# Seven stretches of TensorE's order with leads of their own, in an attention and gated-MLP kernel with packed results and three blocks of maxima on ScalarE and GpSimd

## The chip, the core and the metric

The kernel runs on one core of one Trainium2 chip. A core has TensorE (PE in the profile; PEld is its loading of weights), VectorE (DVE), ScalarE (ACT), GpSimd (POOL) and SyncE (SP), which here issues every DMA. The engines work beside each other and wait for one another through semaphores. Each runs its own instructions in the order in which they were written. The metric is the device time of one execution in microseconds, given as the median of several runs.

## What is computed

A sequence of 2048 tokens of 512 features is normalised, and the result goes both into attention with 32 heads of 16 features and into a gated MLP of width 1792. Both results and the input are added.

```python
def _A_ref(x, wqkv, wo):
    B, S, D = x.shape
    H = 32
    Dh = D // H
    qkv = (lambda x, *d: x.transpose(*d))((x @ wqkv).reshape(B, S, 3, H, Dh), 2, 0, 3, 1, 4)
    q, k, v = qkv[0], qkv[1], qkv[2]
    scores = jnp.einsum("bhqd,bhkd->bhqk", q, k) * (Dh ** -0.5)
    p = _softmax(scores, axis=-1)
    o = jnp.einsum("bhqk,bhkd->bhqd", p, v)
    return (lambda x, *d: x.transpose(*d))(o, 0, 2, 1, 3).reshape(B, S, D) @ wo

def _B_ref(x, w1, w3, w2):
    gate = jnp.einsum("bsd,df->bsf", x, w1)
    up = jnp.einsum("bsd,df->bsf", x, w3)
    h = _silu(gate) * up
    out = jnp.einsum("bsf,fd->bsd", h, w2)
    return out

x = A_x
xn = _layernorm(x, axis=-1)
return x + _A_ref(xn, A_wqkv, A_wo) + _B_ref(xn, B_w1, B_w3, B_w2)
```

## The kernel before

**Tiling.** The 32 heads form 8 groups of four, and the 2048 queries four chunks of 512. A *unit* is one chunk, one group and 256 queries of it, or 128 at the very start and in the last four groups. There are 73 units, 0 to 72, and they are worked in order. A head has 16 features, and each head of a group stands in 32 partitions of its own, so that TensorE works on the four heads in four row groups.

**The two passes over the scores.** The softmax subtracts each row's exact maximum, so the scores are computed twice.

- In the first pass, `p1_cand` (L1052), TensorE computes a *block*: 128 queries against 512 keys for two heads, into two PSUM banks. VectorE reduces the block to two columns of maxima (`part`, L1101). There are 1024 blocks, 16 for a unit of 256 queries. Banks 0 to 3 hold two blocks in turn.
- When a unit's blocks are done, `final_max` makes the row maxima. GpSimd does it in six small operations (L1209 to L1216), or VectorE in one reduction for the first three and the last eight units (L1239). GpSimd then writes the negated maxima into `Z` (L1186, L1188). For most units a transposing DMA makes `Zs` of them, and four small DMAs put the rows beside the queries in `QZ` (L1228). The queries themselves come into `QZ` by four more DMAs (L1061), issued when the units that used the place are through. For the first three and some of the last units TensorE and ScalarE do it instead (tile AQ, L803).
- In the second pass, `p2_cand` (L1344), TensorE computes the scores again, this time with the maximum subtracted by two further rows of the product. ScalarE takes the exponential of a bank of 512 columns into a slot of `PT` (L1360), or of two banks in one instruction (`exp_pair`, L1390). A unit of 256 queries has 32 such tiles, one of 128 has 16.

**Results.** `tile_PV` (L574) multiplies the exponentials with the values. Each head's 16 result rows are followed by a row of sums of the exponentials, and the rest of its 32 partitions is unused. ScalarE copies this to `U` (L1455). A chain normalises it, one unit at a time: a DMA takes the sums out (Lc), GpSimd raises them to the power of -1 (L1480), two DMAs spread the reciprocals over the partitions through DRAM (rd, R), and GpSimd multiplies (L1500) into `onorm`. For the last three units (`FAST_PV`) TensorE also multiplies with ones, and VectorE does a reciprocal and a product (L1445, L1447) instead.

**Output.** `tile_OUT` adds, in one PSUM bank for 128 tokens, the input, 14 products of the MLP and one product for each of the 8 groups with `wo`, whose rows are spread in the same way with zeros between. ScalarE copies the bank out (L912). The last four tiles are split: OUTA holds all but the groups' products, and OUTB those (L588); VectorE adds the two (L957). The MLP's tiles G and U are followed by three ScalarE instructions (L844 to L850) and three of GpSimd (L828 to L833).

**The order.** `_build` simulates the engines with its own costs and writes all instructions in the order it finds. In each step each engine offers its best candidate, and the earliest one is emitted. For TensorE, `pick_pe` weighs a block of the first pass (a), a tile of the second (b) and a matmul of a column tile (c: results, projections, MLP, output). A block is due `A_LEAD` before VectorE will have finished its work, and a score tile `ROW_LEAD` before ScalarE's queue is empty. What isn't due gives way to column work. `COUPLE` lets two of them go together, `RELAX` delays tiles of the second pass, `PAIR_WAIT` is how long ScalarE may wait for a pair, and `PV_LEFT` is how many exponentials of a unit may be open when its results begin. When there is no column work and TensorE's recent load is low, a filler is put in: a product of the identity and `xnT` into a free bank. Work may also be forced ahead when the recent load is too low for the clock. `K.at(LEADS.get(...))` sets these leads anew every 32 blocks (`STRETCH`). `LEADS` is empty, so they are the same throughout. VectorE takes its queue `redq` in order; the last units' reciprocals and OUTB's additions go into the same queue.

## Time and profile before

| | |
|---|---|
| median of 3 runs | 1202.11 us (1200.79 to 1204.87) |
| span of the profiled execution | 1199.6 us |
| VectorE busy, share of the span | 1181.7 us, 99% |
| ScalarE | 1168.2 us, 97% |
| TensorE | 1118.9 us, 93% |
| GpSimd | 442.0 us, 37% |
| granted TensorE clock, mean | 0.998 |

The span is the time from the first to the last instruction on the core; the runs' times lie a little above it. A row of the timeline or the chain begins with the start and the length in us; the number in brackets is the idle time of the engine just before, and what ended it. In the windows view a row is the stretch, its length, the engines' busy time, the granted clock, the DMA share and GB/s. A group row has the busy time and the mean length in ns, then the idle time before. The length of a VectorE or ScalarE instruction overlaps the next one's start, so what counts for a full engine is the pitch, from start to start.

### The profile page before, as it was taken

To read this page: it belongs to the slowest core of one execution; us is meant where nothing else is said; L and a number is where in the kernel's file an instruction comes from. 1 tells how busy PE (TensorE), PEld (TensorE's weight loads), DVE (VectorE), ACT (ScalarE), POOL (GpSimd) and SP (SyncE) were. 2 spreads that over 40 slices of the span, in tenths; PEclk is the share of its full clock that TensorE was granted. 3 is DMA by queue.
4 is the path that set the end of the run, shared out by engine and by line. 5 is a ranking of instruction groups with operands and counts; after the bars stand their busy time and mean duration, and the time that the engine had idled before them with its cause. 6 is when DMAs were issued, how large, how long until landed. Compare 5 with 4: busy or idle time off the path is not lost.

```text
span 1199.6 us, 32809 instructions
## 1 busy us (share of the span) xinstructions
PE 1118.9 (93%) x13295; PEld 489.5 (41%) x13451; DVE 1181.7 (99%) x1087; ACT 1168.2 (97%) x2249; POOL 442.0 (37%) x855
## 2 busy tenths in 40 slices
PE   8999999999899999999999999999999999898997
PEld 3433334334334433333434433433333444345554
DVE  9999999999999999999999999999999999999995
ACT  7879999999999999999999999999999999999997
POOL 3254645532222156542222154356532222233220
PEclk9999999999999999999999999999999999999999
DMA  6523223211011122210001121022110200000000
GB/s 185 120 59 83 70 53 91 58 49 30 20 26 31 42 56 48 55 42 23 24 21 30 33 64 44 24 49 61 39 27 20 59 24 24 20 19 14 13 11 23
DMA packets 136756, 53.54 MB, mean 45 GB/s; under 512 B 102189, under 2 KB 136605, under 8 KB 136605
## 3 DMA queue, kind: packets, MB, share of 16 engines
q1 hardware_dynamic: 136604, 51.44, 17.2%
q8 instruction: 106, 1.74, 0.6%
q14 instruction: 46, 0.37, 0.1%
HBM read 38.86 MB, written 6.74 MB: 38 GB/s over the span
## 4 chain that ended last, share of the span: by engine, by line
ACT 47%; PE 27%; DVE 22%; issue 2%; POOL 1%; DMA 1%; another core or an unknown queue 0%
ACT PT L1360 35%; DVE part L1101 21%; PE ps L588 9%; PE ps L1344 8%; ACT PT L1390 6%; PE ps L574 6%; PE ps L1052 4%; ACT th L844 1%; ACT U L1455 1%; ACT zg L846 1%; ACT ub L850 1%; ACT kq L750 1%; DVE t L615 1%; DVE hT L648 0%; DMA R<-rd 0%
## 5 line engine op out<-in xcount | busy, mean ns | idle before, releaser
L1101 DVE TENSOR_REDUCE part<-ps 128x2 f32<-128x1024 f32 x1024 | 1160.1, 1212 | 1.4 <-PE ps L1344 1.0
L1360 ACT ACTIVATE PT<-ps 128x512 bf16<-128x512 f32 x1714 | 908.8, 651 | 6.4 <-PE ps L1344 2.9
L1344 PE MATMUL ps<-QZ,KT 32*128 32x256 bf16 (+1 forms) x3456 | 526.2, 273 | 15.4 <-ACT PT L1390 5.1
L1052 PE MATMUL ps<-KT,QT 32*128 32x512 bf16 x2048 | 402.2, 385 | 8.4 <-DVE part L1101 4.2
L1344 PEld LDWEIGHTS ps<-QZ,KT 32*128 32x128 bf16 (+1 forms) x3456 | 200.7, 93 | 191.2 <-ACT PT L1360 71.3
L1480 POOL TENSOR_TENSOR Rc<-Lc,mone 128x8 f32<-128x8 f32 (+1 forms) x70 | 105.9, 1513 | 239.9 <-DMA Lc<-U 239.8
L574 PE MATMUL ps<-PT,Vaug 128*17 128x256 bf16 (+1 forms) x4672 | 176.5, 261 | 4.9 <-ACT PT L1390 1.1
L1390 ACT ACTIVATE PT<-ps 128x1024 bf16<-128x1024 f32 x167 | 174.5, 1092 | 1.4 <-PE ps L1344 1.1
L588 PE MATMUL ps<-xnT,w 128*128 128x512 bf16 (+1 forms) x528 | 144.3, 339 | 14.0 <-ACT zg L846 4.8
L1052 PEld LDWEIGHTS ps<-KT,QT 32*128 32x128 bf16 x2048 | 98.5, 91 | 138.7 <-DVE part L1101 80.2
L588 PE MATMUL ps<-xnT,ident 128*128 128x256 bf16 (+1 forms) x400 | 129.4, 345 | 17.6 <-ACT PT L1390 6.9
L574 PEld LDWEIGHTS ps<-PT,Vaug 128*17 128x17 bf16 x4672 | 85.8, 89 | 80.0 <-issue 56.3
L831 POOL TENSOR_TENSOR a<-zg,ub 128x512 f32<-128x512 bf16 x56 | 64.6, 1154 | 72.5 <-ACT ub L850 72.5
L588 PEld LDWEIGHTS ps<-xnT,ident 128*128 128x128 bf16 x484 | 42.3, 96 | 103.5 <-ACT PT L1360 53.8
L1344 PE MATMUL ps<-QT,KT 32*128 32x128 bf16 (+1 forms) x1216 | 80.8, 220 | 3.1 <-ACT PT L1390 1.8
L588 PEld LDWEIGHTS ps<-xnT,w 128*128 128x128 bf16 x557 | 45.0, 97 | 75.3 <-issue 33.8
L588 PE MATMUL ps<-w,hT 128*128 128x512 bf16 (+1 forms) x255 | 69.7, 344 | 2.5 <-ACT U L1455 1.2
L833 POOL TENSOR_TENSOR hT<-a,t 128x512 bf16<-128x512 f32 x56 | 71.0, 1268 | 2.4
L1209 POOL TENSOR_TENSOR mx<-part 128x16 f32<-128x16 f32 (+1 forms) x62 | 13.1, 212 | 154.2 <-DVE part L1101 154.1
L1500 POOL TENSOR_TENSOR wk_on<-U,R 128x256 bf16<-128x256 f32 (+1 forms) x37 | 23.4, 632 | 121.1 <-DMA R<-rd 121.1
L1344 PEld LDWEIGHTS ps<-QT,KT 32*128 32x128 bf16 x1216 | 46.4, 92 | 30.3 <-issue 14.0
L1500 POOL TENSOR_TENSOR on_b<-U,R 128x256 bf16<-128x256 f32 (+1 forms) x33 | 23.5, 711 | 52.2 <-DMA R<-rd 52.1
(92 smaller groups left out, 596.0 us busy)
## 6 DMA issues: line engine op xcount, KB each, us to landing
w<-in_B_w_dram SPq DMA_DIRECT2D x112, 128.0 KB
R<-rd SPq DMA_DIRECT2D x55, 128.0 KB
QT<-qd SPq DMA_DIRECT2D x31, 128.0 KB
KT<-kd SPq DMA_DIRECT2D x28, 128.0 KB
QZ<-QT SPq DMA_DIRECT2D x216, 8.0 KB
QZ<-Zs SPq DMA_DIRECT2D x216, 1.0 KB
xr<-in_A_x_dram SPq DMA_DIRECT2D x16, 128.0 KB
out_dram<-osb SPq DMA_DIRECT2D x16, 128.0 KB
```

Source lines behind the costliest of these rows:

```text
L574: ins = e.matmul(bank(bk)[32 * i:32 * i + m, c0 + a:c0 + b], make_lhsT(i), rhs if (a, b) == (0, ncols) else rhs[:, a:b], start=start, stop ...
L588: return e.matmul(bank(bk)[0:rows, c0 + a:c0 + b], lhsT, rhs if (a, b) == (0, ncols) else rhs[:, a:b], start=start, stop=stop, **kw)
L831: q.append(_Item(lambda e: e.tensor_tensor(a32[:, :], zg[:, ss, :], ub[:, ss, :], ALU.mult), [("zg", ss), ("ub", ss)], [("a32",)], 1.1, 1.25))
L833: q.append(_Item(lambda e: e.tensor_tensor(hT[:, hslot(idx), :], a32[:, :], t1[:, :], ALU.mult), [("a32",), ("t1",)], [("hT", hslot(idx))] ...
L1052: ins = e.matmul(bank(2 * sl + i), QT[32 * j:32 * j + 32, qs, q * 128:(q + 1) * 128], KT[32 * j:32 * j + 32, g, c_ * 512:(c_ + 1) * 512], ...
L1101: redq.append(_Item(lambda e: e.tensor_reduce(dst, pair_ap.rearrange("p (a b) -> p a b", b=512), AX.X, ALU.max), writes, [("part", par, qt ...
L1209: _Item(lambda e: e.tensor_tensor(d2, p4[:, :, 0:2], p4[:, :, 2:4], ALU.subtract), keys, [M0], 0.27),
L1344: ins = e.matmul(bank(b)[:, i * nq:(i + 1) * nq], KT[rows, g, (k0 + i) * 128:(k0 + i + 1) * 128], mov[rows, :], start=True, stop=True, **kw)
L1360: expq.append(_Item(lambda e: e.activation(PT[:, sl, :], bank(b), ACTF.Exp, scale=SCALE), [("ps", b)], [("PT", sl)], _c_act(512), cb=cb, e ...
L1390: return _Item(lambda e: e.activation(PT[:, s0:s1 + 1:s1 - s0, :], ps8[:, b0:b1 + 1:b1 - b0, :], ACTF.Exp, scale=SCALE), [("ps", b0), ("ps ...
L1480: poolq["nrm"].append(_Item(lambda e: e.tensor_tensor(Rc[:, pp, 0:nl], Lc[:, pp, 0:nl], mone[:, 0:nl], ALU.pow), [("Lc", pp), ("mone",)], ...
L1500: poolq["nrm"].append(_Item(lambda e: e.tensor_tensor(onorm[ob][:, g, q0:q0 + nq], U[:, us, 0:nq], R[:, pp, 0:nq], ALU.mult), [("U", us)] ...
```

## The change

- **Bypass.** Units 17, 36 and 38 give up their last block of the first pass. From 12 blocks before the unit's first one, `by_cand` puts its two banks in the place of a second-pass tile, ScalarE copies them to `ST` (in one instruction where `exp_pair` can), and `tree` has GpSimd halve the rows from 512 to 32 columns in four levels of three operations, with VectorE reducing the remaining 2 x 32. The code for a split of blocks, which was switched off, goes.
- **Packing.** The results of two groups stand together in 128 partitions of `onorm`, 64 each, so `wo` is used as it lies in DRAM and an output tile has 4 products of results instead of 8. To move them, `U` goes to DRAM (`ud`) and 16 rows of each head come back (`Uc`); the reciprocals are spread over 64 partitions. The last group of the last chunk stays as it was (`on_l`, `wo_l`), so the last four output tiles have 5 products. The PSUM evacuation to `U` now waits for the copy to DRAM of two units before (`UF`), not for the whole normalisation. GpSimd's operations on the upper partitions are set between waits ("fence").
- **Leads.** `LEADS` has entries for stretches 1, 2, 4, 10, 14, 19 and 31.
- **Tail.** The last units' reciprocals and OUTB's additions go into a queue of their own, `lateq`, used once all reductions are written and the last unit's `Z` is. After the first pass results are preferred by 0.4 us and AQ tiles by 1.0 among column work. In the last 8 blocks no column work is forced for the clock.
- **Buffers.** `PT` has 40 slots instead of 38; `part` has three buffers, and a block of unit u waits for the maxima of unit u-3.

```diff
+        fence = None
+        if eng == "pool" and self.ops[eng] and "fence" in (name, self.last_pool):
+            fence = self.ops[eng][-1]
+        if eng == "pool":
+            self.last_pool = name
...
-    NPT = 38
+    BYPASS = {17: 1, 36: 1, 38: 1}
+    NPT = 40 if BYPASS else 44
...
-    LEADS = {}
+    LEADS = {1: {'A_LEAD': 0.75}, 2: {'PV_LEFT': 4, 'RELAX': 0.0, 'A_LEAD': 0.75}, 4: {'PV_LEFT': 7}, 10: {'A_LEAD': 0.9}, 14: {'COUPLE': 0.16}, 19: {'COUPLE': 0.2, 'PAIR_WAIT': 0.0, 'A_LEAD': 0.8}, 31: {'COUPLE': 0.2}}
...
-        poolq["pad"].append(_Item(lambda e: e.memset(wo[:, :, :], 0.0), [], [("wo",)], 3.5,
+        WOL_KEYS = [("wk0",), ("wq0",), ("wo_l",)]
+        poolq["pad"].append(_Item(lambda e: e.memset(wo_l, 0.0), [], WOL_KEYS, 1.2,
                                   cb=lambda op: late_loads(), pred=lambda: ("AUG", 1) in done))
 
         def late_loads():
+            later_dma(lambda e: e.dma_start(wo[:, :, :], wo_v), [], [("wo",)], lat=4.0)
+            later_dma(lambda e: e.dma_start(wo_l[0:64, 0, :], A_wo[D - 128:D - 64, :]), [], [("wo_l",)])
             for j in range(4):
-                later_dma(lambda e, j=j: e.dma_start(wo[32 * j:32 * j + 16, :, :], wo_v[j]), [("wo",)],
-                          [("wor", j)])
+                later_dma(lambda e, j=j: e.dma_start(wo_l[32 * j:32 * j + 16, 1, :],
+                                                     A_wo[D - 64 + 16 * j:D - 48 + 16 * j, :]), [], [("wo_l",)])
...
+        def on_groups(qc, ts, lo=0, hi=NG, first=False):
             ob = (qc + 1) % 2
-            return (lambda bk: all_groups(bk, onorm[ob][:, g, ts * 128:(ts + 1) * 128], wo[:, g, :], D,
-                                          start=start, stop=stop),
-                    [("ON", ob, g, ts), ("wo",)] + [("wor", j_) for j_ in range(4)], _c_mm(512),
-                    lambda: ("ON", qc, g, ts) in done)
+            last = qc == NQC - 1
+            parts = [((2 * k, 2 * k + 1), onorm[ob][:, k, :], wo[:, k, :], "wo") for k in range(NP - last)]
+            if last:
+                parts += [((NG - 2,), onorm[ob][:, NP - 1, :], wo_l[:, 0, :], "wo_l"),
+                          ((NG - 1,), on_l[:, :], wo_l[:, 1, :], "wo_l")]
+            parts = [x for x in parts if x[0][0] >= lo and x[0][-1] < hi]
+
+            def grp(k, gs, src, w, key):
+                return (lambda bk: all_groups(bk, src[:, ts * 128:(ts + 1) * 128], w, D,
+                                              start=first and k == 0, stop=gs[-1] == hi - 1),
+                        [("ON", ob, g, ts) for g in gs] + [(key,)] + ([("ONz",)] if gs == (NG - 2,) else []),
+                        _c_mm(512), lambda: all(("ON", qc, g, ts) in done for g in gs))
+            return [grp(k, *x) for k, x in enumerate(parts)]
...
+        by_list = []
         for u in range(NU):
-            p1 += p1_list(u)
+            l = p1_list(u)
+            n = BYPASS.get(u, 0)
+            for k in range(n):
+                by_list.append((len(p1),) + l.pop()[1:])
+            p1 += l
...
+            if u >= 3 and ("FM", u - 3) not in done:
+                return None
...
+        by_next = [0]
+        by_free = [True]
+
+        def by_cand():
+            k, h = divmod(by_next[0], 2)
+            if k >= len(by_list):
+                return None
+            n, u, qt, kc, pair = by_list[k]
             qc, g, q0, nq = units[u]
             ug = qc * NG + g
+            j = 2 * pair + h
+            if p1_n[0] < n - BY_LOOK or ("QT", ug) not in done or ("KT", g, kc) not in done:
                 return None
+            if h == 0 and not by_free[0]:
                 return None
             b, b_rd = score_bank(h == 1)
             if b is None or len(p2_busy) >= 4:
                 return None
             qs = ug % 3
             q = q0 // 128 + qt
+            reads = [("QT", qs, q, j), ("QTr0", qs, q), ("QTr1", qs, q)] + kh_keys(g, kc, (j,))
             writes = [("ps", b)]
             rd = P.ready("pe", reads, writes)
             st = P.pe_start("row", (j,), rd)
 
             def emit():
+                by_next[0] += 1
+                by_free[0] = False
                 p2_busy.add(b)
+                P.pe(lambda e: e.matmul(bank(b), QT[32 * j:32 * j + 32, qs, q * 128:(q + 1) * 128],
+                                        KT[32 * j:32 * j + 32, g, kc * 512:(kc + 1) * 512],
+                                        start=True, stop=True, tile_position=(32 * j, 0)),
+                     reads, writes, "row", (j,), _c_mm(512), name="by_%d" % k, first="act")
+                note_load(st, 512)
 
                 def cb(op):
                     p2_busy.discard(b)
+                    if h == 1:
+                        tree(u, qt, kc, pair)
+                expq.append(_Item(lambda e: e.activation(ST[:, h, :], bank(b), ACTF.Identity),
+                                  [("ps", b)], [("ST", h)], _c_act(512), cb=cb, exp=(b, h, None)))
+            return st, emit, rd
+
+        def tree(u, qt, kc, pair):
+            par = u % 3
+            S_ = [("ST", 0), ("ST", 1)]
+            dst = part[:, par, qt, 2 * pair:2 * pair + 2, kc]
+            n = 256
+
+            def rest(op):
+                it = _Item(lambda e: e.tensor_reduce(dst, ST[:, :, 0:BY_END], AX.X, ALU.max), S_,
+                           S_ + [("part", par, qt, 2 * pair + i, kc) for i in range(2)], _c_dve(2 * BY_END), cb=last)
+                if p1_left[u] == 1 or red_n[0] >= NP1:
+                    redq.insert(0, it)
+                else:
+                    pend_fin.append(it)
+
+            def last(op):
+                by_free[0] = True
+                p1_left[u] -= 1
+                if p1_left[u] == 0:
+                    fin = final_max(u)
+                    if fin is not None:
+                        redq.insert(0, fin)
+            while n >= BY_END:
+                a_, b_ = ST[:, :, 0:n], ST[:, :, n:2 * n]
+                tt, ts = 0.11 + 0.0043 * n, 0.1 + 0.002 * n
+                poolq["tree"] += [
+                    _Item(lambda e, a_=a_, b_=b_: e.tensor_tensor(a_, a_, b_, ALU.subtract), S_, S_, tt),
+                    _Item(lambda e, a_=a_: e.tensor_scalar(a_, a_, BIG, 0.0, ALU.min, ALU.max), S_, S_, ts),
+                    _Item(lambda e, a_=a_, b_=b_: e.tensor_tensor(a_, a_, b_, ALU.add), S_, S_, tt,
+                          cb=rest if n == BY_END else None)]
+                n //= 2
...
+                if not flat:
+                    later_dma(lambda e: e.dma_start(ud[pp][:, :, 0:nq], U[:, us, 0:nq]), [("U", us)], [("ud", pp)],
+                              cb=n1b)
+
+            def n1b(op):
+                done.add(("UF", u))
+                later_dma(lambda e: e.dma_start(Uc[c0:c0 + 64, pp, 0:nq], ud[pp][:, 0:16, 0:nq]), [("ud", pp)],
+                          [("Uc", pp)])
...
+                pref = st
+                if p1_n[0] >= NP1:
+                    pref -= PV_AHEAD if t.name.startswith("PV") else AQ_AHEAD if t.name.startswith("AQ") else 0.0
+                if best is None or pref < best[5] - 1e-6:
+                    best = (st, t, reads, writes, g[2], pref)
...
-                        redq.extend(items)
+                        lateq.extend(items)
...
-            d = d_cand()
+            d = by_cand()
             if d is not None:
-                late = (P.free["dve"] + sum(it.occ for it in redq) + 1.13 * (d[3] - p1_n[0] - 1)
-                        - 0.476 * len(expq) - SPLIT_LEAD)
-                rows.append((max(late, d[2]), d))
+                b = d + (None,)
...
-            if recent_cols(c[0], CLOCK_W - K.HORIZON) + ROW_RATE * K.HORIZON < CLOCK_MIN and c[0] <= end + K.URG_WAIT:
+            if p1_n[0] < NP1 - P1_LAST and recent_cols(c[0], CLOCK_W - K.HORIZON) + ROW_RATE * K.HORIZON < CLOCK_MIN and c[0] <= end + K.URG_WAIT:
...
-            for q, depth in ((dveq, 8), (redq, 1)):
+            for q, depth in ((dveq, 8), (redq, 1)) if red_n[0] < NP1 else ((redq, 1), (lateq, "zlast" in done)):
```

286 lines of the change are left out of this document (118 added, 168 removed).

## The prediction

> **What bounds the kernel now.** I read the page first, then VectorE's timeline, the windows view, ScalarE's timeline and the chain.
>
> ```profile
> span 1199.6 us, 32809 instructions
> PE 1118.9 (93%) x13295; PEld 489.5 (41%) x13451; DVE 1181.7 (99%) x1087; ACT 1168.2 (97%) x2249; POOL 442.0 (37%) x855
> ACT 47%; PE 27%; DVE 22%; issue 2%; POOL 1%; DMA 1%; another core or an unknown queue 0%
> ...
> 99.56 141.49 DVE L1101 TENSOR_REDUCE part<-ps 128x2 f32<-128x1024 f32 x125
> ...
> 1171.06 6.87 DVE L1101 TENSOR_REDUCE part<-ps 128x2 f32<-128x1024 f32 x6
> 1178.44 0.96 DVE L1445 RECIPROCAL R<-ps 128x128 f32<-128x128 f32 x1 [0.51 <-PE ps L574]
> 1179.43 0.29 DVE L1447 TENSOR_TENSOR wk_on<-ps,R 128x128 bf16<-128x128 f32 x1
> 1179.64 1.21 DVE L1101 TENSOR_REDUCE part<-ps 128x2 f32<-128x1024 f32 x1
> ```
>
> The reader is to see two full engines. VectorE reduces 125 blocks without a gap in 141.49 us. Taking off the 1.21 us of the last one, the pitch is 140.28/124 = 1.131 us; 1024 of them are 1158 us, nearly the whole span. But its last reduction ends at 1180.85, and the span ends 18.7 us later. What happens then is ScalarE's: the chain gives it 47%, more than VectorE.
>
> ```profile
> 300.00:690.00 390.00, 386.82 (x736) 1.00 0.14 35
> 690.00:750.00 60.00, 58.05 (x115) 1.00 0.23 54
> 750.00:1170.00 420.00, 417.93 (x802) 1.00 0.12 29
> ...
> 681.34 0.38 ACT L1455 ACTIVATE U<-ps 128x256 f32<-128x256 f32 x1 [0.51 <-PE ps L574]
> 682.81 1.02 ACT L1390 ACTIVATE PT<-ps 128x1024 bf16<-128x1024 f32 x1 [1.08 <-PE ps L1344]
> ...
> 722.00 0.38 ACT L1455 ACTIVATE U<-ps 128x256 f32<-128x256 f32 x1 [0.51 <-PE ps L574]
> 723.70 0.60 ACT L844 ACTIVATE th<-ps 128x512 bf16<-128x512 f32 x1 [1.32 <-PE ps L588]
> ...
> 1174.31 3.58 ACT L1360 ACTIVATE PT<-ps 128x512 bf16<-128x512 f32 x7
> 1179.07 2.67 ACT L1360 ACTIVATE PT<-ps 128x512 bf16<-128x512 f32 x5 [1.18 <-PE ps L1344]
> 1193.32 0.60 ACT L1360 ACTIVATE PT<-ps 128x512 bf16<-128x512 f32 x1
> ```
>
> The first three rows are ScalarE's busy time by stretch. It idles 3.18 us from 300 to 690, 1.95 from 690 to 750, and 2.07 in the 420 us after. So from 750 on ScalarE is full, and it finishes at 1193.92, 13.1 us after the last reduction, with about two units of exponentials (31 tiles) run after 1179. **ScalarE's position at 750 us, plus its tail, is the end.** The four bracketed waits at 681 to 724 show the last place where it ran dry: the next unit's scores weren't there. Their supply is seen on Pool and on SP's queue:
>
> ```profile
> 671.79 0.21 POOL L1209 TENSOR_TENSOR mx<-part 128x16 f32<-128x16 f32 x1 [0.72 <-DVE part L1101]
> ...
> 678.09 1.92 SPq L1228 DMA_DIRECT2D QZ<-Zs  x3
> 680.06 2.44 SPq L1061 DMA_DIRECT2D QZ<-QT  x4
> 682.53 0.60 SPq L1228 DMA_DIRECT2D QZ<-Zs  x1
> ```
>
> Unit 36's last reduction releases Pool at 671.79, and its exponentials begin at 682.81, 11 us later: maxima, transpose, four row copies, with four copies of another unit in between (2.44 us). Whatever makes that reduction earlier ends this wait earlier.
>
> **The change, part by part.**
>
> *Three bypassed blocks (units 17, 36, 38).* VectorE loses 3 x 1.131 = 3.39 us and gains three reductions of 64 elements per partition. None is in the trace. The floor is the smallest reduction, which holds the next back by 0.08 us; the ceiling is a 128x512 addition:
>
> ```profile
> 1161.86 0.15 DVE L1239 TENSOR_REDUCE negm<-part 128x4 f32<-128x16 f32 x1
> 1161.94 9.13 DVE L1101 TENSOR_REDUCE part<-ps 128x2 f32<-128x1024 f32 x8
> ...
> 1196.71 0.69 DVE L957 TENSOR_TENSOR osb<-ps,zg 128x512 bf16<-128x512 f32 x1 [0.48 <-remote]
> ```
>
> 64 elements are nearer the first, so 0.13 each, 0.4 together: VectorE is 3.0 us ahead after unit 38. ScalarE gains six copies of a bank, or three of two banks. Two pairs in a row (next fence) take 1.93 us, the last 1.02, so a pair costs 0.91: 3 x 0.91 = 2.7 us. They are issued from 12 blocks before the unit's first, near 296, 639 and 674 us (counted back and on at 1.131 us a block from 671.79, where unit 36's last one is done, no. 575). If all of it goes where ScalarE was idle, its gain at 750 is 3.18 + 1.95 - 2.7 = 2.4 us, which VectorE's 3.0 allows. Bounds: 3.0 gained, or 2.7 lost if no idle time is filled. I take 2.4, because the waits at 681 and 722 come just after two of the copies and at units whose maxima come 2.3 and 3.4 us sooner (two and three blocks less).
>
> Pool gets three trees of 12 operations over two tiles, halved four times. Nearest rows:
>
> ```profile
> L833 POOL TENSOR_TENSOR hT<-a,t 128x512 bf16<-128x512 f32 x56 | 71.0, 1268 | 2.4
> L828 POOL TENSOR_SCALAR t<-th 128x512 f32<-128x512 bf16 x56 | 34.8, 621 | 11.4 <-ACT th L844 8.8 <-POOL hT L833 1.4 <-ACT ub L850 0.2
> L1500 POOL TENSOR_TENSOR on_b<-U,R 128x256 bf16<-128x256 f32 x31 | 22.5, 727 | 52.2 <-DMA R<-rd 52.1
> L1500 POOL TENSOR_TENSOR wk_on<-U,R 128x128 bf16<-128x128 f32 x13 | 5.9, 457 | 45.9 <-DMA R<-rd 45.9
> ...
> 1189.56 1.93 ACT L1390 ACTIVATE PT<-ps 128x1024 bf16<-128x1024 f32 x2
> ```
>
> Two additions and one clamp a level: 2 x 1.27 + 0.62, then 2 x 0.73 + 0.4, 2 x 0.46 + 0.3 and 2 x 0.35 + 0.25 (the clamps and the last size estimated from these rows): 7.1 us a tree. It starts some 13 us before the unit's own reductions and has 30 us before their maxima, so Pool hides it, at nothing; without that cover the maxima are late (rival 3).
>
> The Trainium skill (Perfetto Trace Analysis, Optimizing Scalar/DVE Operations) warns that GpSimd and VectorE share an SBUF read port, so that shifting work between them might not help. By that the trees would hold VectorE up; this is rival 5.
>
> *Packed results.* Each of twelve output tiles needs 4 matmuls of results instead of 8, the last four 5. In the body this buys nothing by itself: TensorE is no bound there, and it runs fillers, whose weights it loads 484 times:
>
> ```profile
> L588 PEld LDWEIGHTS ps<-xnT,ident 128*128 128x128 bf16 x484 | 42.3, 96 | 103.5 <-ACT PT L1360 53.8 <-ACT PT L1390 21.5 <-DVE part L1101 14.0
> ...
> 667.51 0.62 SPq L1476 DMA_DIRECT2D Lc<-U  x1
> ...
> 677.77 0.72 POOL L1500 TENSOR_TENSOR on_b<-U,R 128x256 bf16<-128x256 f32 x1 [3.69 <-DMA R<-rd]
> ```
>
> The price is two more DMAs for 69 units, U to DRAM and back into 64 partitions. Both lie beside the reciprocal's chain, which takes from 667.51 to 677.77, 10 us; SP pays 2 x 0.62 = 1.2 us of issue in 18 us. They are issued behind Lc<-U, after the row copies that ScalarE waits for. Zero, then; uncovered, 1.2 us at each of units 36 and 38. Freeing U earlier, two more PT slots, a third part buffer (with its wait for the maxima of three units before, long done), Pool's fences and the smaller memset touch nothing that is late: zero.
>
> *The tail.* (a) The reciprocal no longer stands before the last reduction: that starts at 1179.64 instead of 1171.06 + 6 x 1.131 = 1177.85, so VectorE gains 1.8 us more. ScalarE has a backlog, so this alone is zero. (b) ScalarE's 1.18 us wait at 1177.89 falls on 104 result matmuls and two fillers:
>
> ```profile
> 1176.82 1.56 PE ps L574 x104
> 1178.38 0.33 PE ps L588 x2
> ...
> 1192.99 1.92 PE ps L574 x128
> ...
> 1194.94 0.97 DVE R L1445
> ```
>
> The fillers are no longer forced in the last eight blocks (0.33), and VectorE's order doesn't hold the last scores. I take 0.7 of 0 to 1.2. (c) The last output tiles lose 12 matmuls between the exponentials. 31 tiles took 1179.07 to 1193.92, 0.479 each; as pairs they would take 0.455, 0.7 less in all: I take 0.4. (d) The last unit's 128 matmuls ran in one piece, from 1192.99, and the reciprocal came 1.02 us after the last exponential. Only the last quarter (0.48 us) needs that one; with results ahead of outputs I take 0.3 of 0 to 0.45.
>
> *The leads* move p1 and result matmuls by 0.05 to 0.2 us, or by one or two exponentials, in seven stretches. VectorE has no gap to fill, so what they can win is ScalarE's idle time. Before 750 that is in the 2.4 already; after it, 2.07 us can be won, or as much lost. One stretch of seven (the last) lies there: I take 0.5.
>
> **Sum:** 2.4 + 0.7 + 0.4 + 0.3 + 0.5 = 4.3 us off the span of 1199.6. The median of the runs, 1202.1, lies 2.5 us above that span; I carry that over: **1197.8 us**.
>
> **Rivals.** (1) *Everything fits*: 3.0 + 1.2 + 0.7 + 0.45 + 2.07 = 7.4 us, 1194.7. For it: the leads work where waits are. Against: 2.07 us after 750 is spread in crumbs. 0.10. (2) *The copies lie on ScalarE's chain*: it pays 2.7 and keeps only the tail's 1.4: 1203.4. For it: ScalarE is busy 99.2% from 300 to 690. Against: the two holes at 681 and 722. SP's 2.5 us for units 36 and 38, if uncovered, gives much the same. 0.14. (3) *Slower: a tree stands before the maxima*. Pool is in order; if trees of units 36 and 38 are released late (copies behind other exponentials), each holds the maxima of its unit or the one before by up to 7.1 us, just where ScalarE has no stock: 1197.8 + 14.2 = 1212. It decides once the two cost over 7.9 us together. For it: unit 35's maxima start at 653.70 (row below), and unit 36's tree, begun near 641 once the copies are made, ends only 6 us ahead of that. Against: Pool was idle before it. 0.08. (4) *It doesn't do what it says*: leads and blocks leave ScalarE's position at 750 alone, only the tail's 1.4 remains: 1200.7. 0.06. (5) *Pool's trees stop VectorE*: 3 x 7.1 = 21 us, 1219. The two rows are Pool's maxima of unit 35, for rival 3, and a stretch of the windows view, which speaks against rival 5:
>
> ```profile
> 653.70 0.21 POOL L1209 TENSOR_TENSOR mx<-part 128x16 f32<-128x16 f32 x1 [1.97 <-DVE part L1101]
> ...
> 810.00:840.00 30.00, 27.75 (x280) 11.13 (x279) 30.00 (x27) 29.97 (x57) 19.63 (x34) 1.00 0.26 59
> ```
>
> In that stretch Pool is busy 19.63 of 30 us and VectorE still 30.00, and the 125 gapless reductions have such Pool work beside them. 0.02. The Trainium skill's own table (SBUF — State Buffer, Who interferes with whom) exempts tensor_reduce on this chip; by that the trace agrees.
>
> **How the numbers follow.** The forecast has 0.60, spread from 1195.5 to 1200.3. A measurement here tells about 0.3%, 3.6 us, from no change, so faster means below 1198.5: that is some 0.38 of the forecast's 0.60 and rival 1, 0.48. Slower is above 1205.7: rivals 3 and 5, 0.10. The rest, 0.42, is the same. The range, 1194.0 to 1203.6, takes in rivals 1, 2 and 4 and leaves out 3 and 5 and a little below.
>
> **What would show it.** 1021 large reductions at a pitch of 1.131 us; no ScalarE wait over 0.5 us at units 36 to 38; ScalarE gapless after 750, ending near 1189.6; the last large reduction near 1176, nothing before it. Wrong if Pool's maxima of units 35 to 38 start more than a microsecond after their last reduction, or if ScalarE's idle time from 300 to 750 stays near 5 us although the copies are there.

## The result, and the profile after

The changed kernel takes 1196.35 us (median of 6 runs, 1194.68 to 1199.05), the kernel before beside it 1202.23 (1200.79 to 1205.85). The ratio is 0.995, with a 95% interval of 0.9936 to 0.9965: 5.9 us less, where 4.3 were forecast. One more run of the kernel before, of 2079.76 us at a granted clock of 1.000, is left out of every figure here, and nothing here explains it.

The page of the changed kernel, from its first line, its busy times and its chain of waits:

```profile
span 1192.7 us, 32937 instructions
PE 1106.1 (93%) x13211; PEld 479.2 (40%) x13360; DVE 1178.7 (99%) x1087; ACT 1169.2 (98%) x2253; POOL 462.6 (39%) x892
ACT 56%; PE 27%; DVE 14%; issue 2%; POOL 1%; DMA 0%; ACTq 0%; another core or an unknown queue 0%
```

The span is 6.9 us shorter. VectorE has 3.0 us less to do and ScalarE 1.0 more, and the chain has moved on to ScalarE: 56% of it now, 47% before; VectorE 14%, 22% before. Where the time came from is seen in ScalarE's windows, first of the kernel before, then of the changed one (stretch, its length, busy time and number of instructions, granted clock, DMA share, GB/s):

```profile
0.00:300.00 300.00, 282.84 (x564) 1.00 0.32 80
...
1170.00:1188.00 18.00, 16.73 (x30) 1.00 0.06 14
1188.00:1200.00 12.00, 5.85 (x9) 0.89 0.11 36
```

```profile
0.00:300.00 300.00, 283.97 (x562) 1.00 0.32 86
300.00:750.00 450.00, 449.00 (x852) 1.00 0.18 45
750.00:1170.00 420.00, 418.99 (x811) 1.00 0.14 36
1170.00:1188.00 18.00, 17.21 (x31) 1.00 0.09 28
```

Length less busy time is idle time. ScalarE's last exponential ends at 1193.92 before and, by a row below, at 1187.30 after.

| ScalarE idle, us | before | after | gained |
|---|---|---|---|
| 0 to 300 | 17.16 | 16.03 | 1.13 |
| 300 to 750 | 5.13 | 1.00 | 4.13 |
| 750 to 1170 | 2.07 | 1.01 | 1.06 |
| 1170 to its last exponential | 1.34 | 0.09 | 1.25 |
| from there to the end of the span | 5.68 | 5.40 | 0.28 |

These gains come to 7.85 us; ScalarE's busy time grew by 0.95 (1168.22 to 1169.17), and 7.85 - 0.95 is the 6.9 us. The largest term is the one that the forecast put first: of the 5.13 us in which ScalarE waited between 300 and 750, one is left. Not all of the 6.9 us is the change, though. The profile of the kernel before has a dip of the granted clock in this row of all engines (busy times of PE, PEld, DVE, ACT, POOL; clock, DMA share, GB/s):

```profile
300.00:330.00 30.00, 26.89 (x266) 10.82 (x271) 29.22 (x27) 29.48 (x51) 7.48 (x18) 0.94 0.08 20
```

VectorE idles 0.78 us there and ScalarE 0.52; the changed kernel's profile has the clock at 1.00 in the same stretch. So up to 0.5 of the 4.13 us, and most of a microsecond of the lead that VectorE has after it, belong to that execution and not to the change. With the clock taken out (next section) the kernels are 5.7 us apart. In the waits view of the changed kernel from 300 to 750 a single line is left:

```profile
ACT PT L1368 <- PE ps L1352: 0.2, 1, 0.2
```

The tail, on VectorE's timeline and then on ScalarE's (start, time, engine, line, tiles, count):

```profile
1168.09 8.00 DVE L1103 TENSOR_REDUCE part<-ps 128x2 f32<-128x1024 f32 x7
1176.13 0.17 DVE L1247 TENSOR_REDUCE negm<-part 128x4 f32<-128x16 f32 x1
```

```profile
1169.87 7.75 ACT L1368 ACTIVATE PT<-ps 128x512 bf16<-128x512 f32 x15
1177.50 0.28 ACT L827 ACTIVATE QT<-ps 128x128 bf16<-128x128 f32 x1
1177.66 3.78 ACT L1368 ACTIVATE PT<-ps 128x512 bf16<-128x512 f32 x7
...
1186.66 0.64 ACT L1368 ACTIVATE PT<-ps 128x512 bf16<-128x512 f32 x1
```

No reciprocal stands among the last reductions, which end at 1176.09 (before: 1180.85), and ScalarE's wait of 1.18 us at 1177.9 is gone. The bypass itself, on Pool's timeline (the beginning of unit 36's tree, and unit 35's maxima) and in the list of groups (busy time, mean ns):

```profile
638.06 1.27 POOL L1176 TENSOR_TENSOR ST<-ST 128x512 f32<-128x512 f32 x1 [0.17 <-ACT ST L1147]
...
651.80 0.22 POOL L1214 TENSOR_TENSOR mx<-part 128x16 f32<-128x16 f32 x1 [1.63 <-DVE part L1103]
```

```profile
L1103 DVE TENSOR_REDUCE part<-ps 128x2 f32<-128x1024 f32 x1021 | 1157.0, 1213 | 1.2 <-PE ps L1068 0.7
L1158 DVE TENSOR_REDUCE part<-ST 128x2 f32<-128x64 f32 x3 | 0.6, 207 | 0.0
L1147 ACT ACTIVATE ST<-ps 128x512 f32<-128x512 f32 x6 | 3.4, 625 | 0.0
L1176 POOL TENSOR_TENSOR ST<-ST 128x512 f32<-128x512 f32 (+3 forms) x12 | 8.3, 693 | 3.0 <-ACT ST L1147 2.3
L1178 POOL TENSOR_TENSOR ST<-ST 128x512 f32<-128x512 f32 (+3 forms) x12 | 8.3, 691 | 1.0
L1177 POOL TENSOR_SCALAR ST<-ST 128x512 f32<-128x512 f32 (+3 forms) x12 | 4.7, 388 | 1.1
```

Three trees take 8.3 + 8.3 + 4.7 = 21.3 us of Pool's time, 7.1 each. VectorE's rows beside the tree that begins at 638.06 are these:

```profile
619.84 27.23 DVE L1103 TENSOR_REDUCE part<-ps 128x2 f32<-128x1024 f32 x24
646.99 0.21 DVE L1158 TENSOR_REDUCE part<-ST 128x2 f32<-128x64 f32 x1
647.11 34.02 DVE L1103 TENSOR_REDUCE part<-ps 128x2 f32<-128x1024 f32 x30
```

With the last one's 1.21 us taken off, the pitch is 26.02/23 = 1.131 us beside the tree and 32.81/29 = 1.131 after it. The Trainium skill (Perfetto Trace Analysis, Optimizing Scalar/DVE Operations) warns that work shifted between VectorE and GpSimd might bring nothing because they share an SBUF read port; the trace shows none of that for these reductions out of PSUM, whose pitch is 1.131 us beside the tree and after it.

### The profile page after: what moved, and what is told of

It reads as the page before. It is cut to its first block, busy times and chain, and to the rows that moved or that the text cites. A ratio compares the mean times of both kernels' runs of the same rounds, so it can differ in the third digit from the quotient of the medians.

```text
span 1192.7 us, 32937 instructions
## 1 busy us (share of the span) xinstructions
PE 1106.1 (93%) x13211; PEld 479.2 (40%) x13360; DVE 1178.7 (99%) x1087; ACT 1169.2 (98%) x2253; POOL 462.6 (39%) x892
## 4 chain that ended last, share of the span: by engine, by line
ACT 56%; PE 27%; DVE 14%; issue 2%; POOL 1%; DMA 0%; ACTq 0%; another core or an unknown queue 0%
ACT PT L1368 40%; DVE part L1103 12%; ACT PT L1398 9%; PE ps L610 9%; PE ps L1352 8%; PE ps L596 6%; PE ps L1068 4%; ACT th L869 2%; ACT zg L871 2%; ACT U L1465 1%; ACT ub L875 1%; ACT kq L772 1%; DVE t L637 1%; DVE hT L670 0%; POOL a L856 0%
## 5 line engine op out<-in xcount | busy, mean ns | idle before, releaser
L1352 PEld LDWEIGHTS ps<-QZ,KT 32*128 32x128 bf16 (+1 forms) x3456 | 197.0, 93 | 188.0 <-ACT PT L1368 68.1
L596 PE MATMUL ps<-PT,Vaug 128*17 128x256 bf16 (+1 forms) x4672 | 183.9, 261 | 5.8 <-ACT zg L871 2.0
L610 PE MATMUL ps<-xnT,ident 128*128 128x512 bf16 (+1 forms) x407 | 136.4, 351 | 26.0 <-ACT PT L1398 13.6
L1352 PE MATMUL ps<-QT,KT 32*128 32x128 bf16 (+1 forms) x1216 | 78.3, 219 | 2.1 <-ACT PT L1398 1.4
L1538 POOL TENSOR_TENSOR wk_on<-Uc,R 64x256 bf16<-64x256 f32 (+1 forms) x36 | 22.8, 632 | 124.8 <-DMA R<-rd 124.1
L1538 POOL TENSOR_TENSOR on_b<-Uc,R 64x256 bf16<-64x256 f32 (+1 forms) x33 | 23.3, 706 | 55.7 <-DMA R<-rd 55.0
```

The source lines that it names most:

```text
L596: ins = e.matmul(bank(bk)[32 * i:32 * i + m, c0 + a:c0 + b], make_lhsT(i), rhs if (a, b) == (0, ncols) else rhs[:, a:b], start=start, stop ...
L610: return e.matmul(bank(bk)[0:rows, c0 + a:c0 + b], lhsT, rhs if (a, b) == (0, ncols) else rhs[:, a:b], start=start, stop=stop, **kw)
L1352: ins = e.matmul(bank(b)[:, i * nq:(i + 1) * nq], KT[rows, g, (k0 + i) * 128:(k0 + i + 1) * 128], mov[rows, :], start=True, stop=True, **kw)
L1538: poolq["nrm"].append(_Item(lambda e: e.tensor_tensor(dst, src, rr, ALU.mult), [key] + RK, on_keys(ob, g, q0, nq), 0.64, cb=cb, name="" if ...
```

## The experiments

**How times are compared.** Single runs of one kernel scatter by 2 to 12 us, and the scatter goes with the mean granted clock that each run lists. Fitted together, the 221 runs of all kernels here that list a clock (each kernel with a level of its own, one slope for all) give 0.82 us for each 0.001 of mean clock, and what is left scatters by 0.6 us. The last column is that level, the time at clock 1.000; its standard error is 0.1 to 0.3 us. It is worked out from the runs, not measured, and it is what tells differences of 1 us. The rounds ran on several chips; given a level of its own on each of the four chips that its runs list, the kernel before lies at 1200.4 to 1200.7, so levels of different rounds can be set side by side. Most expectations were written for medians, with about 1202.1 for the kernel before and 1196.4 for the changed one; they are compared below by their distance from these.

| kernel | runs | median (range), us | ratio to before, 95% | at clock 1.000 |
|---|---|---|---|---|
| before, its runs with a clock | 95 | 1201.87 (1200.50 to 1206.38) | 1 | 1200.6 |
| changed | 6 | 1196.35 (1194.68 to 1199.05) | 0.9950 (0.9936 to 0.9965) | 1194.9, with e13 |
| e1 no leads | 12 | 1200.11 (1199.07 to 1203.68) | 0.9987 (0.9976 to 0.9998) | 1199.5 |
| e3 no bypass | 12 | 1200.94 (1199.48 to 1205.22) | 0.9998 (0.9986 to 1.0010) | 1200.0 |
| e4 tail off | 6 | 1196.61 (1195.97 to 1199.14) | 0.9957 (0.9944 to 0.9971) | 1196.3 |
| e5 packing only | 12 | 1204.00 (1201.34 to 1212.21) | 1.0016 (1.0000 to 1.0033) | 1201.7 |
| e6 bypass late | 11 | 1203.12 (1201.96 to 1208.01) | 1.0016 (1.0005 to 1.0026) | 1202.3 |
| e8 late leads | 11 | 1200.39 (1199.29 to 1204.95) | 0.9994 (0.9983 to 1.0004) | 1198.7 |
| e9 only 19 | 8 | 1198.57 (1197.64 to 1199.19) | 0.9973 (0.9963 to 0.9982) | 1197.5 |
| e10 all but 19 | 12 | 1199.83 (1196.31 to 1202.87) | 0.9978 (0.9964 to 0.9992) | 1195.6 |
| e11 six blocks | 10 | 1202.77 (1200.55 to 1212.77) | 1.0004 (0.9984 to 1.0025) | 1201.1 |
| e12 no 17 | 10 | 1200.33 (1197.87 to 1205.61) | 0.9983 (0.9965 to 1.0000) | 1197.9 |
| e13 changed, again | 5 | 1197.80 (1196.29 to 1200.76) | 0.9962 (0.9947 to 0.9978) | (above) |
| e14 rows first | 11 | 1201.50 (1199.28 to 1205.32) | 1.0004 (0.9991 to 1.0016) | 1199.7 |

### One part taken away at a time

e1 empties the leads:

```diff
-    LEADS = {1: {'A_LEAD': 0.75}, 2: {'PV_LEFT': 4, 'RELAX': 0.0, 'A_LEAD': 0.75}, 4: {'PV_LEFT': 7}, 10: {'A_LEAD': 0.9}, 14: {'COUPLE': 0.16}, 19: {'COUPLE': 0.2, 'PAIR_WAIT': 0.0, 'A_LEAD': 0.8}, 31: {'COUPLE': 0.2}}
+    LEADS = {}
```

> The changed kernel with LEADS empty, all else kept. Theory A (supply: the three bypassed blocks bring the maxima of units 36 and 38 sooner, and ScalarE's position at 750 us follows; the leads only let it follow fully): ScalarE keeps the 2.4 us that the idle time before 750 allows, plus the tail's 1.5, so 3.9 us under the kernel before, about 1198.3. Theory B (the leads carry it): only the tail's 1.5 us is left, about 1200.7. Theory C (packing carries it): as the changed kernel, 1196.4.

e3 takes out the three bypassed blocks and keeps the rest, the 40 slots too:

```diff
-    BYPASS = {17: 1, 36: 1, 38: 1}
-    NPT = 40 if BYPASS else 44
+    BYPASS = {}
+    NPT = 40
```

> The changed kernel with no bypassed block (1024 large reductions again) and 40 slots, leads kept. Theory A: VectorE stands only 1.0 us ahead at unit 38 (that much is the missing stall near 310 us, not the bypass), ScalarE's position at 750 gains 1.0 to 1.9 instead of 4.9, and with the tail's 1.5 the time is about 1199.0; ScalarE's idle time from 640 to 750 comes back to 2 us or more. Theory B: no loss, even a gain of the copies' 2.8 us, 1193.6 to 1196.4. Theory C: as the changed kernel.

e4 puts the tail's order back:

```diff
-    P1_LAST = 8
-    PV_AHEAD = 0.4
-    AQ_AHEAD = 1.0
+    P1_LAST = 0
+    PV_AHEAD = 0.0
+    AQ_AHEAD = 0.0
...
-                        lateq.extend(items)
+                        redq.extend(items)
```

> The changed kernel with the tail's rules undone: reciprocals and OUTB's additions in the common VectorE queue, column work forced to the end, no preference for results or AQ. Theory A: the body is untouched to within 0.3 us at unit 66, and the end loses 1.5 us (1.2 between unit 70 and the last exponential, 0.3 after it): about 1197.9, the last large reduction 1.8 us later. Rival: ScalarE's backlog hides the order, and the time is that of the changed kernel within 0.3 us.

e5 has all three edits at once, so that the packing of the results, with what goes with it, is left alone.

> Packing and the buffers alone: no leads, no bypass, tail rules undone. Theory A: nothing in the body, 12 matmuls less in the tail: 1201.8, between 1200.8 and 1202.8. Theory C (packing carries the gain by freeing TensorE): 3 us or more under the kernel before, under 1199.2.

At clock 1.000 the changed kernel loses 4.6 us without the leads, 5.1 without the bypass and 1.4 without the tail's rules; without all three it loses 6.8. The parts come to 11.1, well over the whole: **bypass and leads need each other.** From e5's 1201.7, leads and tail without bypass (e3) bring 1.7, bypass and tail without leads (e1) 2.2, but bypass and leads (e4) 5.4. If the tail's 1.4 is the same everywhere, which was not tried, leads alone bring 0.3 and the bypass alone 0.8. Beside the kernel before, e1 is 1.1 us faster, which is nearest to its theory B, and e3 about half a microsecond, well short of its theory A's 3.1: neither part carries the gain. Two things stay open. The seven leads are one set, used as it stands in every run; other leads might do more without the bypass. And no run has bypass and leads without the packing, so whether they need it is not shown.

Why is seen on ScalarE. Its timeline in e3:

```profile
684.56 0.38 ACT L1465 ACTIVATE U<-ps 128x256 f32<-128x256 f32 x1 [0.57 <-PE ps L596]
685.82 1.02 ACT L1398 ACTIVATE PT<-ps 128x1024 bf16<-128x1024 f32 x1 [0.87 <-PE ps L1352]
...
727.00 0.39 ACT L1465 ACTIVATE U<-ps 128x256 f32<-128x256 f32 x1 [1.21 <-PE ps L596]
```

With the leads but no bypass, ScalarE runs dry at units 34, 36 and 38 (before: at 36 and 38). The first exponentials of units 34 to 36 come 10.3 to 11.1 us after their last reductions; in none of the profiles do those of units 33 to 36 come sooner than 10.1 us after. So only an earlier reduction would help much, and whatever the leads had won was waited away. In e1 the supply is there, but ScalarE is late by itself: it reaches unit 36 12.7 us after that unit's last reduction, 2.3 us later than the changed kernel, 1.0 of it lost in the first 75 us of this execution. It comes too late to use what VectorE gives. A unit starts at the later of the two, when its scores can be had and when ScalarE is through with the one before; moving either alone stops at the other.

For the tail, the order in which VectorE works is in e4 what it was before:

```profile
1168.53 5.96 DVE L1103 TENSOR_REDUCE part<-ps 128x2 f32<-128x1024 f32 x5
1174.41 0.95 DVE L1455 RECIPROCAL R<-ps 128x128 f32<-128x128 f32 x1
...
1175.60 2.35 DVE L1103 TENSOR_REDUCE part<-ps 128x2 f32<-128x1024 f32 x2
```

The last reduction ends 1.9 us later (1177.94 instead of 1176.09), the last exponential 0.9 us (1188.23), the span 1.3 (1194.0). But 0.4 of each was lost long before, as this execution stands 0.4 us later all the way to unit 70. So the profiles give the tail's rules 0.9 us, 0.5 of it before the last exponential and 0.4 after, and the fit gives 1.4; the medians, 0.3 apart, could not tell it from the rival.

### Where the three blocks lie, and how many

e6 moves them to units where ScalarE has a stock (in the changed kernel their exponentials begin 21 to 25 us after the unit's last reduction, not 10 to 12, so scores are ready and ScalarE does not wait for them):

```diff
-    BYPASS = {17: 1, 36: 1, 38: 1}
+    BYPASS = {44: 1, 46: 1, 48: 1}
```

> The changed kernel with the three bypassed blocks at units 44, 46 and 48 instead of 17, 36 and 38, all else kept. Theory A (the blocks pay because the maxima of units 36 and 38 come sooner, while ScalarE has nothing to do): there ScalarE runs dry at units 34 to 38 as without any bypass, and after 750 us the copies' 2.8 us lie on a full ScalarE, so it is slower than without a bypass (runs with a full head clock there: 1200.4): 1202 to 1203.5. Rival (VectorE's total work decides; where the blocks are does not matter): as the changed kernel, 1196.4.

Windows of ScalarE in e6:

```profile
300.00:690.00 390.00, 386.17 (x719) 1.00 0.17 44
690.00:750.00 60.00, 58.31 (x114) 1.00 0.21 51
```

VectorE is relieved just as much, but the 3.83 and 1.69 us of idle time before 750 are back, and the copies then go on a ScalarE that has none to spare: 1202.3 at clock 1.000, 7.4 us behind the changed kernel and 2.3 behind no bypass at all, near the three copies' 2.7. That is theory A, and place decides.

e12 leaves out one block, e11 has six:

```diff
-    BYPASS = {17: 1, 36: 1, 38: 1}
+    BYPASS = {36: 1, 38: 1}
```

```diff
-    BYPASS = {17: 1, 36: 1, 38: 1}
+    BYPASS = {14: 1, 17: 1, 20: 1, 34: 1, 36: 1, 38: 1}
```

> The bypassed block of unit 17 left out, those of 36 and 38 kept. Theory A (ScalarE had idle time near 300 us with or without that block, and supply and ScalarE's load trade evenly there): VectorE 1.0 us later from unit 17 on, ScalarE 0.9 us less to copy; ScalarE at unit 38 within 0.5 us of the changed kernel, time 1196 to 1197. Rival B (supply alone decides at unit 34, where without any bypass ScalarE ran dry): ScalarE 1.0 us later from unit 34 on, 1197 to 1197.8.

> Six bypassed blocks (units 14, 17, 20, 34, 36, 38) instead of three. Theory A (after the change ScalarE is full from unit 20 on, 0.85 us idle from 300 to 690, so the three bypassed blocks already took all the idle time there was): VectorE 3.0 us earlier still at its last reduction, ScalarE 2 to 2.7 us later from unit 38 on, time 1198 to 1199.5 where the changed kernel has 1196.4. Theory B (VectorE's maxima are still what ScalarE waits for): ScalarE 2 to 3 us earlier, 1193.5 to 1194.5. Rival C (the extra trees come too late on Pool at two neighbouring units): over 1201, with Pool's maxima of units 35 to 38 more than a microsecond after their last reduction.

e12 lost 3.0 us at clock 1.000, more than either theory had for it (at most 0.6 and 1.4). ScalarE's timeline, and below it SP's queue, in e12:

```profile
666.84 0.38 ACT L1465 ACTIVATE U<-ps 128x256 f32<-128x256 f32 x1 [0.89 <-PE ps L596]
668.81 3.73 ACT L1368 ACTIVATE PT<-ps 128x512 bf16<-128x512 f32 x7 [1.58 <-PE ps L1352]
```

```profile
661.41 1.93 SPq L1236 DMA_DIRECT2D QZ<-Zs  x3
...
663.84 3.31 SPq L1077 DMA_DIRECT2D QZ<-QT  x4
667.19 0.60 SPq L1236 DMA_DIRECT2D QZ<-Zs  x1
```

Beside what this execution lost at its head (its first 45 us), VectorE is only 0.9 us later from unit 17 on, yet ScalarE stands 2.5 us before unit 35. The last of the four row copies, with which the unit's scores can begin, went behind four copies of another unit. In the changed kernel the four go in one piece. The unit's exponentials begin 12.2 us after its last reduction, where the changed kernel has 10.4. So supply decided there (rival B), and a late unit seemed to be made later by its own queue; e14 takes that up.

e11 went the way of theory A, at twice its price: 6.3 us over the changed kernel. Two groups of e11:

```profile
L1398 ACT ACTIVATE PT<-ps 128x1024 bf16<-128x1024 f32 x144 | 154.2, 1105 | 0.2
L1147 ACT ACTIVATE ST<-ps 128x512 f32<-128x512 f32 x12 | 6.8, 618 | 1.3 <-PE ps L1137 1.3
```

VectorE's last reduction is no earlier (1175.99): 1.2 us were lost at the head of this execution, and between 250 and 310 it idles 1.6 us, 1.2 of them before the small reductions of two trees, where the changed kernel idles 0.2. So two trees were late on Pool, but not where rival C had them: the maxima of units 35 to 38 begin 0.1 us after their last reductions. ScalarE has six copies more and 25 pairs of exponentials fewer (144, 169 in the changed kernel). Its last exponential ends 7.8 us later, at 1195.11: 3.9 us are more work (1173.1 us busy, 1169.2 in the changed kernel), 1.2 the head, and the rest waits elsewhere, 1.3 of them for the scores of its copies (row above). Here the extra copies gave ScalarE more work and waits than the sooner maxima took away.

### Which leads

e8 leaves out the first two stretches, e9 keeps only stretch 19, e10 all but that one:

```diff
+    LEADS = {4: {'PV_LEFT': 7}, 10: {'A_LEAD': 0.9}, 14: {'COUPLE': 0.16}, 19: {'COUPLE': 0.2, 'PAIR_WAIT': 0.0, 'A_LEAD': 0.8}, 31: {'COUPLE': 0.2}}
```

```diff
+    LEADS = {19: {'COUPLE': 0.2, 'PAIR_WAIT': 0.0, 'A_LEAD': 0.8}}
```

```diff
+    LEADS = {1: {'A_LEAD': 0.75}, 2: {'PV_LEFT': 4, 'RELAX': 0.0, 'A_LEAD': 0.75}, 4: {'PV_LEFT': 7}, 10: {'A_LEAD': 0.9}, 14: {'COUPLE': 0.16}, 31: {'COUPLE': 0.2}}
```

> The changed kernel without the leads of stretches 1 and 2 (56 to 128 us), the others kept. Theory A: the early leads' 5 us of ScalarE are used up by unit 25 but some 1.9 us of them still stand at unit 34, and are needed to follow the sooner maxima: 1197.5 to 1198.5. Rival (what is won before the empty stretch at 680 is lost there): 1196.4, as the changed kernel.

> The changed kernel with the leads of stretch 19 alone (708 to 744 us, units 38 and 39). If the leads' gain of 3.5 us comes from that stretch, where the kernel without leads falls back from 3.5 to 2.4 us ahead between units 38 and 39: 1197.0 to 1198.2. If it comes from the early ones: 1199.5 to 1200, as without leads.

> The changed kernel with all leads but those of stretch 19. The counterpart: if stretch 19 carries the gain, 1198.5 to 1200; if the early leads do, 1196.4 to 1197.5.

At clock 1.000, with 1199.5 for no leads and 1194.9 for all: stretch 19 alone brings 2.0 us, but only 0.7 are lost when it alone is taken out; the five late ones together bring 0.8, less than one of them alone. e8 missed its forecast: it lies 3.8 us over the changed kernel, where theory A had 1.1 to 2.1. e9 falls between its two answers. e10's median, 3.5 over the changed kernel's, would say that stretch 19 carries the gain; but half of its runs have clocks of 0.992 or 0.993, and the 0.7 at clock 1.000 says that the early leads carry most of it. Each lead changes the whole order behind it, so the seven have no single prices. What the early ones do is seen by counting ScalarE's instructions off in the trace. At units 6 to 9 the changed kernel's exponentials are some 5 us ahead of before, with seven to nine other instructions fewer done (92 against 100 at unit 6). At unit 24 they are level, with six more done, two of them the copies of unit 17; at unit 30 they are 2.4 us ahead, with just these two more. So the early leads put exponentials first and the other work later. What that saves is idle time: between 355 and 630 ScalarE idles 0.2 us in the changed kernel and in e10, and 1.4 to 1.7 in e1, e8 and e9, the three without the early leads (before: 0.9).

### Is it SP's order that makes the supply late?

e14 is e3 (no bypass) with the four row copies put at the head of SP's queue when they are made:

```diff
-                    for j in (2, 3, 0, 1):
+                    for k, j in enumerate((2, 3, 0, 1)):
                         later_dma(lambda e, j=j: e.dma_start(
                             QZ[32 * j + 16:32 * j + 18, j, q0:q0 + nq], Zs[32 * j + 16:32 * j + 18, par, 0:nqt, :]),
                             [("Zs", par)], qz_keys(j, "a", q0, nq),
                             cb=(lambda op: done.add(("AUG", u))) if j == 1 else None,
-                            pred=lambda: "QZ" in done and p2_units_done[0] > qz_prev[u])
+                            pred=lambda: "QZ" in done and p2_units_done[0] > qz_prev[u]); spq.insert(k, spq.pop())
```

> No bypassed block, all leads and the tail's rules, as in e3, and one edit more: the four row copies QZ<-Zs of a unit, for which its exponentials wait, go to the head of SP's queue when they are made, so that the four copies QZ<-QT of another unit no longer stand in between them. In e3 those stood ahead of the last row copy at exactly the three units where ScalarE ran dry (34, 36, 38), for 1.8 to 2.6 us. Theory A' (the supply is short only because of that order; a late unit is made later by it): the waits of 1.4 us each at units 34, 36 and 38 shrink to under 0.4, ScalarE is 3 to 4 us earlier than e3 from unit 38 on, time at full clock 1196 to 1197.5 where e3 has 1200.0. Rival D (the order is only a sign that ScalarE has caught up; the supply is bound by VectorE's maxima and the transpose): the waits stay over 1 us each, 1199.5 to 1200.5. Rival E (the new plan's order of TensorE costs or gains more than the rows): ScalarE's offset to e3 changes by over 1.5 us before unit 30, and the time follows that.

SP's queue at unit 36 in e3, in e14 and in the changed kernel:

```profile
679.49 1.93 SPq L1236 DMA_DIRECT2D QZ<-Zs  x3
681.52 2.52 SPq L1077 DMA_DIRECT2D QZ<-QT  x4
684.09 0.60 SPq L1236 DMA_DIRECT2D QZ<-Zs  x1
```

```profile
679.08 2.51 SPq L1236 DMA_DIRECT2D QZ<-Zs  x4
681.69 2.43 SPq L1077 DMA_DIRECT2D QZ<-QT  x4
```

```profile
674.07 2.53 SPq L1236 DMA_DIRECT2D QZ<-Zs  x4
676.64 3.67 SPq L1077 DMA_DIRECT2D QZ<-QT  x4
```

The order is now the changed kernel's, but the time stays where it was: 1199.7 against e3's 1200.0. Between 630 and 760 ScalarE still idles 4.8 us (e3: 5.2), though no longer in waits of over 1 us at each of the three units, as rival D had it. The first exponentials of units 34 and 36 come 10.4 and 10.5 us after their last reductions instead of 11.1, so the queue's order costs some 0.6 us a unit there, not the 1.4 of the waits. At unit 38 the four copies of the other unit went out before the row copies were there at all. Theory A' falls for these units; that the order is mostly a sign that ScalarE has caught up (rival D) is what is left, and is argued, not shown. What makes unit 36's rows ready 5.0 us sooner in the changed kernel (674.07 instead of 679.08) is the earlier reduction (5.6 us); 3.9 us of that are e14's low clock at its head.

### The changed kernel once more

> The changed kernel once more, beside these two on the same chip, for its scatter: 1194.7 to 1199 in single runs, the longer ones those with a granted clock below 0.999; median 1196 to 1197.

Its runs had clocks of 0.993 to 0.998 and took 1196.29 to 1200.76, so the median of 1197.80 lies over the expected 1196 to 1197; at clock 1.000 they agree with the first six within 0.2 us. No kernel here beats the changed one: e10 and e4 come nearest, 0.7 and 1.4 us behind.

## Why the prediction held, point by point

- **What bounds the kernel: right.** ScalarE's waits before 750 and its tail were the end. Removing the waits moved the end (5.13 to 1.00 us, the largest term); relieving VectorE elsewhere did not (e6, e11).
- **The first term, 2.4 us, was too small, and so was the whole.** It was 5.13 of idle time filled, less 2.7 for copies. Of the idle time 4.13 was gained, and 1.13 more before 300, where nothing had been priced. ScalarE's busy time rose by 0.95 instead of 2.7, though the copies, which ran as six single ones and not as three pairs, alone show 3.4: the rest of its work took less, which no run here explains. 4.13 + 1.13 - 0.95 = 4.3 instead of 2.4 is the term that was mis-sized; up to 0.5 of it is the dip of the clock in the profile before. The other 3.8 are 1.4 more than 2.4, and 1.4 is also what the whole sum lacks at clock 1.000 (4.3 forecast, 5.7 by the fit). The reason, that the waits come at units whose maxima come sooner, holds (e3, e6, e12). What the step left out is that the leads had to bring ScalarE there in time: without them (e1) 4.6 us are gone at clock 1.000, where the forecast left only 0.5 to them by themselves.
- **VectorE's 3.0 us: right.** A small reduction holds the next back by 0.12 us (646.99 to 647.11), 0.13 had been taken. At unit 38 VectorE was 4.0 us ahead, 1.0 more, as its gaps between 247 and 311 are smaller; 0.78 of that is the idle time in the clock's dip before, and not the change. The 1.0 was lost again by unit 67.
- **The trees: right**, 7.1 us each, hidden on Pool. Unit 36's tree was done by 646.99, when VectorE reduced its result, and unit 35's maxima began only at 651.80. Rival 3 had no ground; rival 5 neither, by the pitch of 1.131 us.
- **Packing at zero: nearly.** e5 is 1.1 us slower than before at clock 1.000 (ratio 1.0000 to 1.0033), its median above the 1200.8 to 1202.8 that were expected, and TensorE's 59 fewer weight loads (13392 against 13451) bought nothing by themselves. (TensorE's busy times on the two pages, 1118.9 and 1106.1, cannot be set side by side: the changed kernel's page has 13360 weight loads but 13211 matmuls, so some matmuls have no record, and e5's, with all 13392, has 1147.8 us.) Where the 1.1 lies was not found; e5's profile was taken in an execution with a low clock at its head. In it ScalarE idles 1.15 us more than before between 630 and 760, which may be the same 1.1 or not.
- **The tail: right in size, as far as it can be told**, 1.4 forecast, 1.4 by e4 at clock 1.000 and 0.9 by its profile (0.3 by the medians, whose ranges overlap). Its wait term, taken at 0.7, was 1.25 by the windows; the 0.28 after the last exponential matches the 0.3 for (d). The 0.4 for fewer output matmuls was not seen apart.
- **The 0.5 for leads after 750: right.** ScalarE idles 2.07 us from 750 to 1170 before, 1.59 in e1, without leads, and 1.01 in the changed kernel; so 0.58 of the 1.06 gained came with the leads.
- **The step from span to median** was carried over at 2.5 us. It came out as 3.7 (1196.35 less 1192.7), as the profiled execution was the fastest of the six.
- **Rivals.** (1) asked for 7.4 us off the span; 6.9 came, and 5.7 at clock 1.000: the outcome lies between it and the forecast. (2), the copies on ScalarE's chain, is what e6 built, and its 1203.4 is near e6's 1203.12. (4) is answered by the windows.
- **What would show it.** 1021 reductions at 1.131 us, the last one done at 1176.09, nothing before it, no wait over 0.5 us at units 36 to 38: all so. After 750 ScalarE was nearly gapless (1.01 us idle). Its end was put near 1189.6 and came at 1187.30.

## What to carry to other kernels

Where two engines are both full, look for the few units at which the one still waits for the other, and bring relief just ahead of those; the same relief elsewhere only moves work onto an engine that has no room. Two remedies for one wait can each be worth little alone and much together, since a unit starts at the later of supply and readiness: test them together and apart before dropping either. (Here one set of leads was tested.) And when single runs scatter by more than the effect, list the granted clock beside each time, and that of the profiled stretch beside each gap, before believing either.

## What the runs showed of the hardware

The granted clock, not the program, makes most of the scatter. The two profiles of the changed kernel are of the same instructions in the same order, 6.1 us apart in span (1192.7 and 1198.8). Windows of all engines, first of the one, then of the other (busy times of PE, PEld, DVE, ACT, POOL; granted clock, DMA share, GB/s):

```profile
880.00:910.00 30.00, 27.01 (x319) 11.38 (x324) 30.00 (x28) 29.96 (x57) 7.73 (x21) 1.00 0.11 30
1010.00:1040.00 30.00, 26.98 (x319) 11.42 (x319) 30.00 (x28) 29.66 (x50) 8.94 (x25) 1.00 0.11 30
```

```profile
880.00:910.00 30.00, 27.03 (x287) 10.95 (x290) 28.89 (x26) 29.03 (x53) 9.98 (x22) 0.94 0.10 27
1010.00:1040.00 30.00, 27.04 (x281) 10.61 (x281) 27.47 (x25) 27.33 (x47) 7.40 (x19) 0.89 0.11 31
```

In the second the clock falls to 0.94 and 0.89 in these stretches. TensorE is as busy and gets less done (287 and 281 matmuls instead of 319), and VectorE and ScalarE, all but gapless in the first, lose 0.9 to 2.5 us a stretch. In e5's profile the dip lies at the head, before any stock has built up:

```profile
20.00:30.00 10.00, 9.10 (x53) 3.53 (x52) 8.84 (x12) 8.01 (x15) 0.49 (x1) 0.72 0.21 60
30.00:40.00 10.00, 10.00 (x44) 3.18 (x42) 7.87 (x8) 4.13 (x7) 0.66 (x3) 0.76 0.27 75
```

VectorE ends the reductions of unit 3 there 4.3 us later than in the profile of the kernel before, and the span is 4.2 us longer. Over all runs 0.001 of mean clock, which is 1.2 us of a 1200 us span, cost 0.82 us. The Trainium skill (TensorE: Matmul & The Clock Gate, Terms) puts the penalty of a throttled clock at about the throttled time times the missing share. By that, as an estimate, 0.001 would cost 1.2 us; the runs here show about two thirds of it. Why one execution of a program has such a dip and another has none was not tried.
